# State turned in place by VectorE, S of ten pieces in pairs, spreading on 256 columns: one change to a chunked attention and two feed-forward layers

## The chip, the core and the metric

The kernel runs on one core of a Trainium2 chip. Its engines work side by side, each through its own list of instructions in order: TensorE (PE; its weight loads are a row of their own, PEld), VectorE (DVE), ScalarE (ACT), GpSimd (POOL) and SyncE (SP, which here only starts DMA transfers). Semaphores tie the lists together. Matrix products are written to PSUM, which has eight banks of 512 fp32 columns; everything else lies in SBUF. The metric is the time of the whole program on the device in microseconds (us), lower is better.

## The reference, cut to what matters

```python
def _attn_ref(x, a, B, C):            # x [4, 8, 768, 32], a [4, 8, 768], B, C [4, 8, 768, 16]
    ...
    for c in range(nc):               # chunks along the sequence
        ...
        L = np.exp(cum[:, :, :, None] - cum[:, :, None, :]) * causal
        CB = np.einsum('bhin,bhjn->bhij', Cc, Bc)
        y_intra = np.einsum('bhij,bhjd->bhid', CB * L, xc)
        y_inter = np.einsum('bhin,bhnd->bhid', Cc, state) * decay_to_i[:, :, :, None]
        ...
        state = decay_full[:, :, None, None] * state + np.sum(Bx, axis=2)

def _moe_ref(x, w_in, w_out):         # x [3072, 256], w_in [256, 2048], w_out [2048, 256]
    h = x @ w_in
    return (h * (1.0 / (1.0 + np.exp(-1.702 * h)))) @ w_out

def _moe2_ref(x, w_in, w_out):        # the same shapes
    h = x @ w_in
    return (h * np.clip(h + 3.0, 0.0, 6.0) / 6.0) @ w_out
```

The output of the attention (4 x 768 tokens of 8 x 32 numbers) goes through the first feed-forward layer and its result through the second.

## The kernel before

**Attention in pieces.** The sequence is cut into 8 chunks of 96 positions; a piece q is one chunk c = q // 4 of one batch row b = q % 4, so there are 32. Each has eight heads, in two groups g of four. The state is carried by 16 extra columns and rows: E = 96 + 16 = 112. A piece needs, for each g: the decays `l` of 112 x 448 (a scan on DVE, L406); the products C times B, called S (`s_mm`, L477: four small matmuls for each g), into one PSUM bank per g; their product `gm` (L480 on DVE, or ACT's copy L483 and POOL's product L487); and then y (`y_mm`, L498: eight matmuls over `gm` and `xs`, the piece's x with the state below it in rows 96 to 111). ACT copies the state's part of y to `st_sb` (L502) and the rest to `xt` (L512); DVE adds what the fp32r copy lost (L516).

**S.** For pieces 0 to 15 the operands of S have 16 rows in fp32. Each g and each batch row of a pair lies at its own 32 partitions (`r = 64 * (b % 2) + 32 * g`), and one piece's two groups are issued in turn. Later pieces have 128 rows in bf16.

**Spreading.** For pieces 0 to 5 the decays' factors come from one fp32 tile of 128 x 224 (`acl`): a matmul whose left operand is one column, repeated 112 times, spreads one row over all partitions (`a_spread`, L394), four such matmuls for a piece, into the `acc` banks. For later pieces a DMA does it (L400).

**State from chunk to chunk.** After a chunk's last piece DVE turns the whole `st_sb` in blocks of 32 x 32 into `st_tr` (L523), and four DMAs of 16 KB carry it to rows 96 to 111 of the next chunk's `xs` (`st_move`, L527).

**The two layers.** The 3072 tokens make six blocks of 512 columns. A unit is one block k, one layer (A or B) and one slice m of 128 of the 2048 hidden numbers, 192 in all. A unit has 12 fp32r matmuls of 512 columns: six for h (L659: the weights' high parts `wh`, then their low parts `wl`) and, two units later, six into two `acc` banks (L698). Block 0 needs pieces 0 to 5. Pieces 6 to 15 run between the units of A0 and A1, the rest later.

**Weights.** 32 slices of 512 KB come packed as 64-bit numbers (`raw`, three buffers, L303); ACT scales them (L309) and makes their low bits (L315), DVE joins them (L321), ACT rounds to `wh` (L324), POOL subtracts to `wl` (L330).

**PSUM.** `h` has 2 banks, `acc` 4, `s` and `y` one each. Pieces 0 to 5 use the two `h` banks for S.

**Order.** Every operation is entered with an engine, an estimated duration, a key (its due time) and the buffers that it reads and writes. `Schedule.run` replays the estimates, takes buffers from the pools in the order of the keys, and so fixes the order of the instructions on each engine. `START` is the due time of the first unit, `PIECE` that of each piece. All DMAs except six at the start are issued by SP, in order, and each of those waits for its own condition at the head of the queue.

Of the kernel before, what the change touches and what calls it, by code (L numbers as in the profile page):

```python
# [22 lines left out]
CH = 96  # L23
# [15 lines left out]
DECB = 2  # L39
SPREAD = 6  # L40
KEEP = ((21, 4), (26, 5))
LAG = 2
START = 25.0
# [11 lines left out]
def SBANK(q, g):  # L55
    if q < 6:
        return f"h:s{q}.{g}"
    return f"{('s', 'y' if 8 <= q < 16 else 'acc')[g]}:s{q}.{g}"


def YBANK(q):
    return f"{'ysysys'[q] if q < 6 else 's' if 8 <= q < 16 else 'y'}:y{q}"


def PIECE(q, lead):

# [150 lines left out]
def ssd_moe_kernel(ctx: ExitStack, tc: tile.TileContext, xs, aa, bc, bcz_d, bc0, wu, pat, idn, out):  # L217
# [23 lines left out]
    w_hi = [const.tile([128, UW], F32R, name=f"wh{p}") for p in range(2 * NM)]  # L241
# [7 lines left out]
    eye2 = late_p.tile([128, NH], F32, tag="eye2", name="eye2")  # L249
# [9 lines left out]
    xs_b = bufs("xs", 2, [E, NB, NH * D], F32)  # L259
# [41 lines left out]

    def w_load(p):
        nc.sync.dma_start(out=B_(f"raw:{p}").rearrange("p n t -> p (n t)"), in_=wu[p].bitcast(U32))  # L303

    def w_scale(p):


        top = B_(f"raw:{p}")[:, :, 1].bitcast(F32)
        nc.scalar.activation(top, top, AF.Prelu, scale=2.0 ** 16, alpha=2.0 ** 32)  # L309

    def w_low(p, act):
        low = B_(f"raw:{p}")[:, :, 0]
        if act:

            nc.scalar.activation(low, B_(f"raw:{p}").bitcast(U8)[:, :, 3], AF.Copy, scale=1 / 32, bias=-31 / 64)  # L315
        else:
            nc.vector.tensor_scalar(low, low, 29, None, ALU.logical_shift_right)

    def w_join(p):
        t = B_(f"raw:{p}")  # L320
        nc.vector.scalar_tensor_tensor(B_(f"dec:{p}"), t[:, :, 1], 3, t[:, :, 0], ALU.logical_shift_left, ALU.bitwise_or)  # L321

    def w_top(p, e):
        (e.copy if e is nc.scalar else e.tensor_copy)(w_hi[p], B_(f"dec:{p}").bitcast(F32))  # L324
# [15 lines left out]
    def more_eye():  # L340

        nc.gpsimd.tensor_tensor(out=eye2, in0=idn_sb[:, 0:NH], in1=idn_sb[:, NS + 1:NS + 2].to_broadcast([128, NH]), op=ALU.mult)
# [22 lines left out]
    add("POOL", 0.2, -30, more_eye, r=["idn"], w=["eye2"])  # L365
    add("-", 0.0, -95, lambda: None, w=["late"])
# [8 lines left out]

    def a_all():
# [6 lines left out]

    def a_store():
        nc.sync.dma_start(out=acl_d.rearrange("r (q f) -> (r q) f", q=4), in_=acl())

    def a_spread(q, g):

        f = acl()
        ps = B_(f"acc:l{q}.{g}")[0:E, 0:4 * E]  # L390
        for i in range(2):
            j = 4 * q + 2 * g + i
            row = idn_sb[:, NS + NH + j:NS + NH + j + 1] if j < NS else eye2[:, j - NS:j - NS + 1]
            nc.tensor.matmul(out=ps[:, 2 * E * i:2 * E * i + 2 * E], lhsT=row.to_broadcast([128, E]),  # L394
                             rhs=f, start=True, stop=True)
# [7 lines left out]
    def decay(q, g):  # L403
        t = B_(lname(q)).rearrange("p h e -> p (h e)")[:, 4 * E * g:4 * E * g + 4 * E]
        a = B_(f"acc:l{q}.{g}")[0:E, 0:4 * E] if q < SPREAD else t
        nc.vector.tensor_tensor_scan(t, a, pat_sb, 0.0, ALU.mult, ALU.add)  # L406
# [58 lines left out]
    def s_mm(q, gs):  # L465
        c, b = divmod(q, NB)
        for k in range(4):
            for g in gs:
                ps = s_bank(q, g)
                if c in ROWS:  # L470
                    t = rows16(c)
                    r, i = 64 * (b % 2) + 32 * g, 4 * (b // 2) + k
                    l, r = t[r:r + NS, 0, i], t[r:r + NS, 1, i]
                else:
                    t = B_(f"st:{c}.{b // 2}").rearrange("p (h s b e) -> p h s b e", h=NH, s=2, b=2)
                    l, r = t[:, 4 * g + k, 0, b % 2], t[:, 4 * g + k, 1, b % 2]
                nc.tensor.matmul(out=ps[:, k, :], lhsT=l, rhs=r, start=True, stop=True)  # L477
# [14 lines left out]
    def y_mm(q):  # L492
        c, b = divmod(q, NB)
        yv, x = y_view(q), B_(f"xs:{c}")
        for g in range(2):
            for k in range(4):
                h = 4 * g + k
                nc.tensor.matmul(out=yv[32 * k:32 * k + 32, g, :], lhsT=x[:, b, h * D:(h + 1) * D],  # L498
# [23 lines left out]
    def st_turn():  # L522
        nc.vector.transpose(st_tr.rearrange("p b g e -> p (b g e)"), st_sb.rearrange("p b g e -> p (b g e)"))  # L523
# [297 lines left out]
```

## Time and profile before

| | |
|---|---|
| runs | 602.7, 604.74, 605.6 us; median 604.74 |
| profiled execution | 602.65 us, of which the span of its instructions is 600.5 |
| PE busy | 590.2 us, 98% of the span |
| ACT, DVE, POOL busy | 315.9, 283.5, 196.2 us |
| units: matmuls of 512 columns | 2304 |
| first unit's first matmul | 29.58 us after the span's start |

"Busy" is time in which an engine has an instruction in it. A matmul's recorded length overlaps the next one's, so what one matmul takes is read from the distance between the starts of two. "Idle before" names what ended an engine's wait. [...]

### The profile page before, as it was taken

To read this page: it belongs to the slowest core of one execution; us is meant where nothing else is said; L and a number is where in the kernel's file an instruction comes from. 1 tells how busy PE (TensorE), PEld (TensorE's weight loads), DVE (VectorE), ACT (ScalarE), POOL (GpSimd) and SP (SyncE) were. 2 spreads that over 40 slices of the span, in tenths; PEclk is the share of its full clock that TensorE was granted. 3 is DMA by queue.
4 is the path that set the end of the run, shared out by engine and by line. 5 is a ranking of instruction groups with operands and counts; after the bars stand their busy time and mean duration, and the time that the engine had idled before them with its cause. 6 is when DMAs were issued, how large, how long until landed. Compare 5 with 4: busy or idle time off the path is not lost.

```text
span 600.5 us, 8563 instructions
## 1 busy us (share of the span) xinstructions
PE 590.2 (98%) x3260; PEld 473.4 (79%) x3260; DVE 283.5 (47%) x404; ACT 315.9 (53%) x594; POOL 196.2 (33%) x161
## 2 busy tenths in 40 slices
PE   8799999999999999999999999999999999999997
PEld 6577778778888887777788888778888888888885
DVE  5786776554443454685642364633322222322221
ACT  2478756667767545455344554434544443544443
POOL 3343420124443635463000573000445000444542
PEclk9989999999999999999999999999999999999999
DMA  8386650432231567468340060420000100000101
GB/s 172 110 258 203 207 146 29 137 107 78 99 106 52 145 177 180 148 172 235 104 142 1 11 165 19 137 62 1 1 0 1 35 1 1 0 2 0 37 0 35
DMA packets 46808, 52.82 MB, mean 88 GB/s; under 512 B 26784, under 2 KB 38416, under 8 KB 46768
## 3 DMA queue, kind: packets, MB, share of 16 engines
q1 hardware_dynamic: 45920, 51.93, 30.2%
q10 hardware_dynamic: 848, 0.35, 0.3%
q8 instruction: 25, 0.41, 0.3%
q14 instruction: 15, 0.12, 0.1%
HBM read 41.21 MB, written 10.60 MB: 86 GB/s over the span
## 4 chain that ended last, share of the span: by engine, by line
PE 92%; DMA 4%; ACT 1%; DVE 1%; SPq 0%; issue 0%; POOL 0%; ACTq 0%; DVEq 0%
PE h L659 44%; PE acc L698 43%; PE s L477 2%; PE y L498 2%; DMA raws<-in_wu 1%; PE s L498 1%; DMA xs<-in_xs 1%; DMA out<-gg 1%; DMA late<-in_bcz 1%; PE acc L477 1%; DMA xs<-st_tr 0%; SPq L527 0%; POOL wl L330 0%; DVE l L406 0%; ACT raws L315 0%
## 5 line engine op out<-in xcount | busy, mean ns | idle before, releaser
L684 POOL TENSOR_TENSOR gl<-gg,gh 128x512 fp32r<-128x512 f32 x95 | 126.8, 1338 | 280.6 <-ACT gh L674 262.6
L659 PE MATMUL h<-xt,wh 128*128 128x512 f32 x768 | 211.1, 397 | 0.9 <-DVE xt L516 0.9
L659 PEld LDWEIGHTS h<-xt,wh 128*128 128x128 f32 x768 | 142.9, 189 | 33.5 <-issue 2.1
L698 PE MATMUL acc<-gh,wh 128*128 128x512 f32 x384 | 149.9, 390 | 0.0
L679 DVE SCALAR_TENSOR_TENSOR gg<-gg,h 128x512 f32<-128x512 f32 x96 | 65.8, 685 | 140.6 <-ACT gg L672 140.4
L698 PE MATMUL acc<-gl,wh 128*128 128x512 f32 x384 | 120.3, 389 | 0.0
L684 DVE TENSOR_TENSOR gl<-h,gh 128x512 fp32r<-128x512 f32 x96 | 66.1, 688 | 110.1 <-ACT gh L674 108.6
L670 ACT ACTIVATE h<-h 128x512 f32<-128x512 f32 x96 | 55.9, 582 | 106.9 <-PE h L659 106.8
L698 PE MATMUL acc<-gh,wl 128*128 128x512 f32 x276 | 109.6, 397 | 0.0
L672 ACT ACTIVATE gg<-h 128x512 f32<-128x512 f32 x96 | 57.4, 598 | 82.6 <-PE h L659 77.7
L659 PE MATMUL h<-xt,wl 128*128 128x512 f32 x276 | 86.3, 394 | 0.6 <-POOL wl L330 0.6
L674 ACT CAST gh<-gg 128x512 fp32r<-128x512 f32 x96 | 59.6, 621 | 51.0 <-DVE gg L679 50.9
L698 PEld LDWEIGHTS acc<-gl,wh 128*128 128x128 f32 x384 | 72.1, 188 | 15.5 <-DVE gl L684 0.2
L698 PEld LDWEIGHTS acc<-gh,wh 128*128 128x128 f32 x384 | 72.1, 188 | 14.3
L406 DVE TENSOR_TENSOR_SCAN l<-l,pat_sb 112x448 f32<-112x448 f32 x52 | 66.6, 1290 | 5.1 <-DMA l<-acl_d 5.0
L659 PEld LDWEIGHTS h<-xt,wl 128*128 128x128 f32 x276 | 52.1, 190 | 12.3 <-POOL wl L330 1.0
L698 PEld LDWEIGHTS acc<-gh,wl 128*128 128x128 f32 x276 | 51.8, 188 | 12.4 <-issue 1.5
L330 POOL TENSOR_TENSOR wl<-dec,wh 128x512 fp32r<-128x512 f32 x23 | 32.7, 1428 | 82.7 <-ACT wh L324 82.7
L674 ACT CAST gh<-h 128x512 fp32r<-128x512 f32 x96 | 56.5, 588 | 3.5
L698 PE MATMUL acc<-gh,w_late 128*128 128x512 f32 x108 | 42.4, 392 | 0.0
L659 PE MATMUL h<-xt,w_late 128*128 128x512 f32 x108 | 33.3, 389 | 0.0
L480 DVE TENSOR_TENSOR gm<-s,l 112x448 f32<-112x448 f32 x26 | 16.1, 619 | 17.3 <-PE s L477 8.2
(76 smaller groups left out, 393.1 us busy)
## 6 DMA issues: line engine op xcount, KB each, us to landing
raws<-in_wu SPq DMA_DIRECT2D x21, 512.0 KB, 5.4
l<-acl_d SPq DMA_DIRECT2D x26, 392.0 KB, 5.6
st<-scr SPq DMA_DIRECT2D x8, 896.0 KB, 5.8
raw<-in_wu SPq DMA_DIRECT2D x11, 512.0 KB, 3.4
scr<-tsplit SPq DMA_DIRECT2D x32, 168.0 KB, 2.7
xs<-in_xs SPq DMA_DIRECT2D x8, 384.0 KB, 6.1
scr<-tsplit SPq DMA_DIRECT2D x16, 112.0 KB, 2.6
raw<-in_bc SPq DMA_DIRECT2D x4, 384.0 KB, 5.6
```

Of the source, the lines that this page charges most:

```text
L330: e.tensor_tensor(out=w_lo[p], in0=B_(f"dec:{p}").bitcast(F32), in1=w_hi[p].bitcast(F32), op=ALU.subtract)
L406: nc.vector.tensor_tensor_scan(t, a, pat_sb, 0.0, ALU.mult, ALU.add)
L477: nc.tensor.matmul(out=ps[:, k, :], lhsT=l, rhs=r, start=True, stop=True)
L480: nc.vector.tensor_tensor(out=B_(f"gm:{q}.{g}"), in0=s_bank(q, g), in1=B_(lname(q))[:, 4 * g:4 * g + 4], op=ALU.mult)
L498: nc.tensor.matmul(out=yv[32 * k:32 * k + 32, g, :], lhsT=x[:, b, h * D:(h + 1) * D], rhs=B_(f"gm:{q}.{g}")[:, k, :], start=True, stop=True)
L659: nc.tensor.matmul(out=ps, lhsT=w[p][:, 128 * j:128 * j + 128], rhs=x[:, xp, j, 0:n], start=not lo and (xp, j) == (1, 0), stop=lo and j == 1)
L670: nc.scalar.activation(ps, ps, AF.Gelu_apprx_sigmoid)
L672: nc.scalar.activation(B_(f"gg:{u}")[:, 0:n], ps, AF.Relu, bias=3.0)
L674: nc.scalar.copy(B_(f"gh:{u}")[:, 0:n], ps if kind == "A" else B_(f"gg:{u}")[:, 0:n])
L679: nc.vector.scalar_tensor_tensor(out=g, in0=g, scalar=6.0, in1=B_(f"h:{u}")[:, 0:n], op0=ALU.min, op1=ALU.mult)
L684: e.tensor_tensor(out=B_(f"gl:{u}")[:, 0:n], in0=g, in1=B_(f"gh:{u}")[:, 0:n].bitcast(F32), op=ALU.subtract)
L698: nc.tensor.matmul(out=acc[d], lhsT=w[p][:, 256 + 128 * d:384 + 128 * d], rhs=g, start=(m == 0 and d not in seen), stop=(m == NM - 1 and d ...
```

## The change

Four things, and what goes with them:

- **The state is turned in place.** `xs` gets 128 partitions. For each half of a chunk (two pieces) DVE turns four blocks of 32 partitions of `st_sb` straight into rows 96 to 127 of the next chunk's `xs`: eight small turns for a chunk where one large turn and four DMAs were. `y_mm` reads rows 0 to 111.
- **S of pieces 6 to 15 in pairs.** `s_mm` takes two pieces, (6,7) to (14,15), and issues their four groups in turn: four different sets of rows, four banks (`s`, `y`, two `acc`). For this the odd piece's S is made with the even one's, and its y alternates between `y` and `s`. Pieces 0 to 5 keep the `h` banks.
- **Spreading on 256 columns.** DVE splits `acl` into an fp32r part and a remainder, each padded by POOL to 256 columns; each row is spread by two fp32r matmuls of 256 columns that add up. POOL makes the fp32r selectors from the constants.
- **Early weights.** Four more raw buffers (`early`, the place of the last eight `wh`) take slices 3 to 6; slices 0 to 6 get earliest times `WAFTER`. `START` goes from 25 to 21, which moves the due times of units and weights.

`HALVES`, `PATQ`, `LOWPS` and their branches are switched off (no unit is halved, no pattern copied). The order of the 192 units stays.

```diff
-START = 25.0
+START = 21.0
...
     if q < 6:
         return f"h:s{q}.{g}"
-    return f"{('s', 'y' if 8 <= q < 16 else 'acc')[g]}:s{q}.{g}"
+    if q < 16:
+        return f"{('sy', ('acc', 'acc'))[q % 2][g]}:s{q}.{g}"
+    return f"{('s', 'acc')[g]}:s{q}.{g}"
...
+EARLY = 8
+WAFTER = (2.9, 4.9, 6.9, 11.0, 13.0, 15.0, 17.0)
+PAIRS = (6, 8, 10, 12, 14)
...
+    def a_part(i):
+        t = B_("gh:acl")[:, 256 * i:256 * i + 2 * E]
+        f = acl()
+        if i:
+            nc.vector.tensor_tensor(out=t, in0=f, in1=B_("gh:acl")[:, 0:2 * E].bitcast(F32), op=ALU.subtract)
+        else:
+            nc.vector.tensor_copy(t, f)
...
-            nc.tensor.matmul(out=ps[:, 2 * E * i:2 * E * i + 2 * E], lhsT=row.to_broadcast([128, E]),
-                             rhs=f, start=True, stop=True)
+            for part in range(2):
+                nc.tensor.matmul(out=ps[:, 2 * E * i:2 * E * i + 256], lhsT=sel[:, j:j + 1].to_broadcast([128, E]),
+                                 rhs=B_("gh:acl")[:, 256 * part:256 * part + 256], start=part == 0, stop=part == 1)
...
-    def s_mm(q, gs):
-        c, b = divmod(q, NB)
+    def s_mm(qs, gs):
         for k in range(4):
-            for g in gs:
+            for q in qs:
+                c, b = divmod(q, NB)
+                for g in gs:
...
-    def st_move(c, k):
-        dst = B_(f"xs:{c + 1}")[CH:E].rearrange("n b (g k d) -> n k (b g) d", g=2, k=4)
-        nc.sync.dma_start(out=dst[:, k], in_=st_tr[32 * k:32 * k + NS].rearrange("n b g d -> n (b g) d"))
+    def st_turn(c, j, k):
+        dst = B_(f"xs:{c + 1}")[CH:128, 2 * j:2 * j + 2].rearrange("n b (g k d) -> n k (b g) d", g=2, k=4)
+        nc.vector.transpose(dst[:, k], st_sb[32 * k:32 * k + 32, 2 * j:2 * j + 2].rearrange("p b g e -> p (b g) e"))
...
-        if b == 3 and c + 1 < NC:
-            add("DVE", 0.45, t + 2.5, st_turn, r=[f"st_sb{i}" for i in range(NB)], w=["st_tr"])
+        if b % 2 and c + 1 < NC:
+            for k in range(4):
+                add("DVE", 0.22, t + 2.4 + 8 * (q == 3), st_turn, c, b // 2, k, r=[f"st_sb{b - 1}", f"st_sb{b}", f"xs:{c + 1}"], w=[f"xs:{c + 1}.{b // 2}.{k}"])
```

Three places show how the instructions move. In the names, the number behind an underscore is the tile's own and differs between the two programs.

SP at the start, from the first `xs` on. Before:

```order
L409 DMA xs_141<-in_xs 96x1024
L409 DMA xs_142<-in_xs 96x1024
L385 DMA acl_d<-gg_147 128x224
L449 DMA late<-in_bc 16x1792 x4
L303 DMA raw_130<-in_wu 128x1024
L303 DMA raws<-in_wu 128x1024 x2
L527 DMA xs_142<-st_tr 16x8x32 x4
L400 DMA l_136<-acl_d 112x896
```

And now:

```order
L453 DMA xs_134<-in_xs 96x1024
L324 DMA raw_123<-in_wu 128x1024
L425 DMA acl_d<-gg_140 128x224
L324 DMA raws<-in_wu 128x1024
L493 DMA late<-in_bc 16x1792 x4
L453 DMA xs_135<-in_xs 96x1024
L324 DMA raws<-in_wu 128x1024
L324 DMA early<-in_wu 128x1024 x4
L440 DMA l_129<-acl_d 112x896
```

Weight 0 stands ahead of the B and C of chunk 1 (`late<-in_bc`) and of the second `xs`, weight 1 ahead of both; four more weights follow at once, where the four `xs<-st_tr` stood, which are gone.

ACT at the start, after the table's load. `gm` is the copy of S (for POOL's product), `st_sb` and `xt` are the copies of y, `raw`, `raws` and `early` the weights. Before:

```order
L483 COPY gm_138<-h_159 112x448
L483 COPY gm_140<-h_158 112x448
L502 COPY st_sb<-y_165 128x2x16
L512 CAST xt_144<-y_165 128x2x96
L483 COPY gm_138<-h_159 112x448
L502 COPY st_sb<-s_164 128x2x16
L512 CAST xt_144<-s_164 128x2x96
L309 ACTIVATE raw_130<-raw_130 128x512
L315 ACTIVATE raw_130<-raw_130 128x512
L309 ACTIVATE raws<-raws 128x512
```

And now, first the beginning:

```order
L528 COPY gm_131<-h_152 112x448
L330 ACTIVATE raw_123<-raw_123 128x512
L340 ACTIVATE raw_123<-raw_123 128x512
L547 COPY st_sb<-y_158 128x2x16
L557 CAST xt_137<-y_158 128x2x96
L528 COPY gm_133<-h_151 112x448
L330 ACTIVATE raws<-raws 128x512
L340 ACTIVATE raws<-raws 128x512
L528 COPY gm_131<-h_151 112x448
```

and then the end of it, up to the copies of pieces 4 and 5:

```order
L330 ACTIVATE early<-early 128x512
L340 ACTIVATE early<-early 128x512
L330 ACTIVATE early<-early 128x512
L340 ACTIVATE early<-early 128x512
L547 COPY st_sb<-y_158 128x2x16
L557 CAST xt_137<-y_158 128x2x96
L352 CAST wh_73<-dec_126 128x512
L330 ACTIVATE early<-early 128x512
L547 COPY st_sb<-s_157 128x2x16
L557 CAST xt_137<-s_157 128x2x32
```

Weight 0's two steps stood behind the copies of piece 1 and now stand ahead of those of piece 0; weights 3, 4 and the first step of 5 stand ahead of the copies of pieces 4 and 5.

PE at the first S behind the units' start. Before, piece 6 alone, in two banks:

```order
L659 MATMUL h_159<-xt_144,wl_107 128x512 x2
L477 MATMUL s_164<-late 112x112
L477 MATMUL acc_162<-late 112x112
L477 MATMUL s_164<-late 112x112
L477 MATMUL acc_162<-late 112x112
```

And now pieces 6 and 7, in four:

```order
L751 MATMUL acc_154<-gl_147,wh_74 128x512
L522 MATMUL s_157<-late 112x112
L522 MATMUL y_158<-late 112x112
L522 MATMUL acc_155<-late 112x112
L522 MATMUL acc_156<-late 112x112
```

Two groups in turn have become four, and piece 7's own S further on is gone.

## Rows read from the trace of the kernel before

**Rows 1.** The page: the span, the granted clock in 40 slices.
```profile
span 600.5 us, 8563 instructions
PEclk9989999999999999999999999999999999999999
```

**Rows 2.** The page: busy us of each engine, share of the span, instructions.
```profile
PE 590.2 (98%) x3260; PEld 473.4 (79%) x3260; DVE 283.5 (47%) x404; ACT 315.9 (53%) x594; POOL 196.2 (33%) x161
```

**Rows 3.** Chain of waits up to 31 us and from 40: start, us, what.
```profile
9.80 8.61 DMA raws<-in_wu
...
25.57 1.96 DMA xs<-st_tr
...
45.52 1.36 PE h L659 x6
```

**Rows 4.** Timeline of PE from 10.9 us: start, us, engine line, op, count.
```profile
10.92 1.77 PE L394 MATMUL acc<-gg,idn_sb 128*112 128x224 f32 x8
12.62 1.04 PE L477 MATMUL h<-late 16*112 16x112 f32 x16
13.59 0.59 PE L498 MATMUL s<-gm,xs 112*32 112x112 f32 x16
14.11 1.77 PE L394 MATMUL acc<-gg,idn_sb 128*112 128x224 f32 x8
```

**Rows 5.** Timeline of DVE up to 30 us.
```profile
5.08 2.07 DVE L406 TENSOR_TENSOR_SCAN l<-acc,pat_sb 112x448 f32<-112x448 f32 x2 [1.46 <-PE acc L394]
...
8.78 2.07 DVE L406 TENSOR_TENSOR_SCAN l<-acc,pat_sb 112x448 f32<-112x448 f32 x2 [0.48 <-PE acc L394]
...
22.85 0.33 DVE L516 TENSOR_TENSOR xt<-s,xt 128x192 fp32r<-128x192 f32 x1
23.10 0.43 DVE L523 STREAM_TRANSPOSE st_tr<-st_sb 128x256 f32<-128x256 f32 x1
...
24.43 1.12 DVE L480 TENSOR_TENSOR gm<-h,l 112x448 f32<-112x448 f32 x2
25.48 0.67 DVE L321 SCALAR_TENSOR_TENSOR dec<-raw 128x512 uint32<-128x512 uint32 x1
```

**Rows 6.** Timeline of ACT: the wait for weight 0.
```profile
15.97 0.67 ACT L309 ACTIVATE raw<-raw 128x512 f32<-128x512 f32 x1 [1.32 <-DMA raw<-in_wu]
```

**Rows 7.** Stretches: busy us of PE, PEld, DVE, ACT, POOL, granted clock, DMA, GB/s.
```profile
0.00:10.00 10.00, 8.27 (x54) 6.18 (x56) 4.25 (x7) 2.02 (x3) 3.13 (x9) 1.00 0.78 153
10.00:20.00 10.00, 10.00 (x120) 8.02 (x116) 8.38 (x12) 4.64 (x13) 2.67 (x3) 1.00 0.80 211
30.00:40.00 10.00, 10.00 (x34) 7.48 (x33) 7.33 (x9) 6.65 (x13) 2.27 (x2) 0.75 0.98 287
```

**Rows 8.** Timeline of PE from the first unit to 42.5 us: S of piece 6 within.
```profile
29.58 2.07 PE L659 MATMUL h<-xt,wh 128*128 128x512 f32 x4 [0.87 <-DVE xt L516]
...
34.89 1.26 PE L659 MATMUL h<-xt,wh 128*128 128x512 f32 x4
...
39.19 1.07 PE L659 MATMUL h<-xt,wh 128*128 128x512 f32 x4
...
41.53 0.34 PE L477 MATMUL s<-late 16*112 16x112 f32 x1
...
42.31 0.26 PE L477 MATMUL acc<-late 16*112 16x112 f32 x1
42.50 1.20 PE L659 MATMUL h<-xt,wh 128*128 128x512 f32 x4
...
43.99 0.39 PE L698 MATMUL acc<-gh,wl 128*128 128x512 f32 x1
```

**Rows 9.** Timeline of PEld in the same S: the weight loads.
```profile
42.02 0.17 PEld L477 LDWEIGHTS s<-late 16*112 16x112 f32 x1
42.02 0.17 PEld L477 LDWEIGHTS acc<-late 16*112 16x112 f32 x1
```

More of the change, by code (lines that the diff above doesn't have):

```diff
@@ L364, in ssd_moe_kernel @@
     add("POOL", 0.3, -90, zero_state, w=["st_sb"])
-    add("POOL", 0.2, -30, more_eye, r=["idn"], w=["eye2"])
-    add("-", 0.0, -95, lambda: None, w=["late"])
+    add("POOL", 0.35, -75, selectors, r=["idn"], w=["sel"])
+    add("-", 0.0, -95, lambda: None, w=["late", "early"])
     add("ACT", 0.1, -91, consts, 1, w=["pat"], kb=100)
@@ L405, in decay, with pat_copy @@
         a = B_(f"acc:l{q}.{g}")[0:E, 0:4 * E] if q < SPREAD else t
-        nc.vector.tensor_tensor_scan(t, a, pat_sb, 0.0, ALU.mult, ALU.add)
+        m = B_("acc:pat")[0:E, 0:4 * E] if SPREAD <= q < PATQ else pat_sb
+        nc.vector.tensor_tensor_scan(t, a, m, 0.0, ALU.mult, ALU.add)
+    def pat_copy():
+        nc.scalar.copy(B_("acc:pat")[0:E, 0:4 * E], pat_sb)
     def x_load(c):
@@ L543, in ssd_moe_kernel @@
         add("POOL", 0.3, t + 0.5, identities, s, r=["idn", "split0"], w=[f"split{s + 1}"])
+    if PATQ > SPREAD:
+        add("ACT", 0.55, kp[SPREAD - 1], pat_copy, r=["pat"], new=["acc:pat"])
     for q in range(NC * NB):
@@ L580, in ssd_moe_kernel @@
         if b == 0 and c > 0:
-            add("SP", 0.4, t - 12, x_load, c, new=[f"xs:{c}"], kb=393)
-        if b == 0 and c > 0:
-            for k in range(4):
-                add("SP", 0.4, t - 3, st_move, c - 1, k, r=["st_tr", f"xs:{c}"], w=[f"xs:{c}.{k}"], kb=16)
+            add("SP", 0.4, t - 12, x_load, c, new=[f"xs:{c}"], kb=393, after=8.0)
         if q < SPREAD:
@@ L587, in ssd_moe_kernel @@
             for g in range(2):
-                add("PE", 0.75, t - 1 + 0.1 * g, a_spread, q, g, r=["gg:acl", "idn", "eye2"], new=[f"acc:l{q}.{g}"])
+                add("PE", 0.48, t - 1 + 0.1 * g, a_spread, q, g, r=["gh:acl", "al", "sel"], new=[f"acc:l{q}.{g}"])
             for g in range(2):
@@ L593, in ssd_moe_kernel @@
             for g in range(2):
-                add("DVE", 1.06, t + 0.1 * g, decay, q, g, r=[lname(q), "pat"] + ["late"] * (q == 3), w=[f"l{q}.{g}"], port=True)
+                add("DVE", 1.06, t + 0.1 * g, decay, q, g, r=[lname(q), "acc:pat" if q < PATQ else "pat"], w=[f"l{q}.{g}"], port=q >= PATQ)
         for g in range(2):
@@ L687, in l2 @@
     def l2(u):
-        kind, k, m = order[u]
-        n = WID[k]
+        kind, k, m, a, b = order[u]
+        n = b - a
         p = m + (NM if kind == "B" else 0)
         hi, lo = B_(f"gh:{u}")[:, 0:n], B_(f"gl:{u}")[:, 0:n]
-        acc = [B_(f"acc:{kind}{k}.{d}")[:, 0:n] for d in range(2)]
+        acc = [B_(f"acc:{kind}{k}.{d}")[:, a:b] for d in range(2)]
         seq = [(d, w, g) for d in range(2) for w, g in ((w_lo, hi), (w_hi, hi))] + [(d, w_hi, lo) for d in range(2)]
@@ L741, in ssd_moe_kernel @@
         acc = [f"acc:{kind}{k}.{d}" for d in range(2)]
-        add("PE", 6 * mm(k), tu[u + LAG] + 0.6, l2, u, r=W + [f"gh:{u}", f"gl:{u}"], **({"new": acc} if m == 0 else {"w": acc}))
+        add("PE", 6 * mm(n), tu[u + LAG] + 0.6, l2, u, r=W + [f"gh:{u}", f"gl:{u}"], **({"new": acc} if m == 0 and lo == 0 else {"w": acc}))
         if m == NM - 1:
```

159 lines of the change are left out of this document (93 added, 66 removed).

## The prediction

> **What bounds the kernel now.** I read the page first: the span is 600.5 us [rows 1], and TensorE has an instruction in it for 98% of it [rows 2]. A share of busy time doesn't say that PE runs at its pace, so the timeline and the chain of waits come next. Six matmuls of 512 columns take 1.36 us where nothing disturbs them [rows 3], 0.227 each; 2304 of them are 522 us. What lies beside that is what a change can take: a start of 29.58 us before the first unit [rows 8], the pieces' own matmuls, and a few waits. The rest of the span is PE at its pace, so there work that is taken off PE is time gained, and work added to the other engines costs only where PE comes to wait for it.
>
> The start has three limits that lie close together. On PE one piece takes 3.19 us from one spreading to the next: 1.70 spreading, 0.97 S, 0.52 y [rows 4]. On DVE it takes two scans (2.07 with overlap, 2.0 net), one product (0.53) and one remainder (0.25), 2.8 us [rows 5]. And ACT, in order, stands still for weights: weight 0 lands at 15.97 [rows 6], weight 1 at 18.41 [rows 3], and the copies of y and S behind them wait too. At the end comes the state: y of piece 4 needs the four DMAs that carry it, and the last of them lands at 27.53, 2.0 us after DVE's last product of piece 5 [rows 3, 5]. Then the first two units run at the granted clock 0.50: from 29.58 to 34.89 they take 5.31 us [rows 8] instead of 2 x 1.36, 2.6 lost; the clock is 0.75 over 30 to 40 us [rows 7] and 1.0 in nearly every slice after that [rows 1].
>
> **The change part by part. The start.** The DMAs of the state go, and those 2.0 us with them; the spreading gets shorter. A spread row takes two matmuls of 256 columns where it took one fp32 matmul of 224 (two records of 0.21). No row shows 256 columns in fp32r; they cost between half of 0.227 (0.113) and the whole, and I take 0.12, since the columns set a matmul's pace in rows 3 and 4. Then a piece's eight take about 1.15 us instead of 1.70, and PE needs 2.65 us for a piece: DVE is last.
>
> So I add up DVE. The first scan began at 5.08 [rows 5]. Two instructions are new ahead of the first spreading (a cast and a subtraction of 224 columns, some 0.3 each by the remainder's 0.33); the first four matmuls are shorter: 5.3. Up to the last product of piece 5 come 12 scans of 1.0, seven products of 0.53, four remainders of 0.25, two joins of 0.6 (moved ahead; 0.67 with overlap) and four turns. A turn of 32 x 128 isn't in the trace; the large one took 0.43 for 256 columns [rows 5], so it costs between 0.2 and 0.43; I take 0.2, by the columns. That is 12.0 + 3.7 + 1.0 + 1.2 + 0.8 = 18.7: 24.0 if DVE never waits.
>
> It will wait, through ACT. Weight 0 is issued three transfers earlier: 112 KB, 448 KB and 384 KB now come behind it, which at the 211 GB/s of 10 to 20 us [rows 7] is 4.5 us, so it lands at 11.5 instead of 15.97. But its two steps stand on ACT ahead of the copies of piece 0's y and piece 1's S. S of piece 2 then begins at 13.6, and DVE stands some 0.8 us for piece 0's remainder and 0.4 for piece 2's product, then 0.3 or so twice: 1.6 in all, 25.6 for the last product. Behind it come y of piece 5 (0.5), piece 4's remainder, four more turns, a join and piece 5's remainder: 27.4. ACT reads the same: weight 2 lands where it did (before 20.2), weights 3, 4 and 5 follow at 512 KB each, at 211 to 287 GB/s 1.8 to 2.4 us apart, so 5 lands near 26; its first step (0.6) and the copy of piece 5's y (0.3) end at 27.0, the remainder at 27.3. **First unit at 27.5: 2.1 us gained.** The bounds: 26.0 with no wait on DVE; 31.9 if weights come at the 153 GB/s of the first 10 us [rows 7], which puts weight 5 at 30.2.
>
> The half clock behind it I leave as it is, 2.6 us: PE has even less to do between S of piece 5 and the first unit than before. Bounds 0 and twice that.
>
> **Pairs of S.** One piece's S takes 0.97 us, and the unit behind it 1.49 from 42.50 to 43.99 instead of 1.36 [rows 8]: 1.10 in all, ten times. Inside, two groups start together, every 0.1 us eight times [rows 8], and so do their weight loads [rows 9]. With four sets of rows the eight rounds should stay, with four matmuls in each. Y is the nearest case that has four at once (four sets of columns): 16 records in 0.52 us [rows 4], four every 0.13. I take 1.13 for a pair, so 2.20 - 1.13 = 1.07 saved, five times: **5.3 us**. If only two go at once, there are 16 rounds: 1.10 + 0.78 = 1.88, 0.3 saved, 1.6 in all.
>
> [...] No run here shows four row tiles yet.
>
> **Early weights.** The fourth unit's first layer took from 39.19 to 41.53, 2.34 us instead of 1.36, since its `wl` was late [rows 8]. Weight 3 lands near 22 now instead of behind the state's DMAs at SP's head. **1.0 us gained**; the later waits for weights are too small to see.
>
> **What is added elsewhere.** Eight turns for one in each of seven chunks, 8 x 0.2 - 0.43 = 1.2 us of DVE for a chunk; after the start DVE has the slack (47% busy over the span [rows 2]), so nothing. S of piece 11 is now made with piece 10's, ahead of A1's first two units, and holds two `acc` banks until DVE has multiplied it; A1's second layer needs those banks. PE gets there some 51 us after the first unit with DVE's work up to that product at about 42 us: it fits, but in order, so I charge **0.5 us** (0 to 2). SP loses 28 transfers; the queue behind them only gets earlier.
>
> **The sum.** -2.1 - 5.3 - 1.0 + 0.5 = -7.9 us. Against the profiled execution: 602.65 - 7.9 = 594.8. That execution is 2.1 us below the median of 604.74, and it is the median that I forecast: 604.74 - 7.9 = **596.8 us**.
>
> **Rivals.**
>
> *ACT's queue is held by the weights.* Weights 3, 4 and 5 now stand ahead of the copies that the first unit needs; before, ACT's waits for weights 0 and 1 were on the chain up to the first unit [rows 3, 6]. At 153 GB/s the first unit starts at 31.9, 2.3 later than before instead of 2.1 earlier: 601.2; somewhat faster transfers give 599 to 601. For it: rows 6. Against it: 287 GB/s between 30 and 40 us, when weights made most of the traffic [rows 7]. I say 600.
>
> *The pairs don't do what they say:* two groups at a time, from the rows of the array or from the weight loads, of which the trace shows two every 0.1 us and never more [rows 9]. 1.6 instead of 5.3: 600.5.
>
> *The clock falls inside the start,* because PE now waits there. It stayed at 1.00 while PE was 83% and 100% busy [rows 7]. If it falls at about 18 us, S of piece 5 and y of pieces 4 and 5 take twice as long on the way to the first unit, some 1.5 us: 598.3. [...]
>
> *Slower: the four loads of a round go in line.* If each held the array for its whole recorded 0.17 us [rows 9], a pair would take 32 x 0.17 + 0.13 = 5.6 instead of 2.2: 17 us more in five pairs, 619. It decides from 0.08 us a load (a pair of 2.7), where it eats the other gains. Against it: two loads fit in 0.1 us now.
>
> **How the numbers follow.** Chances: the forecast 0.60, ACT held 0.17, pairs of two 0.10, clock 0.09, loads in line 0.04. About 0.5% (3 us, below 601.7) is what a measurement of this kernel can tell from no change. The forecast and the clock are faster; of ACT held and the pairs of two about a fifth ends above 601.7. So faster 0.90, same 0.06, slower 0.04. The range: at the low end a first unit at 26.0 and a half clock that costs 1 us less with no wait at A1, 593.8, and a base like the lowest run, 2.0 less: 592; at the high end the two middle rivals with a little over: 601.5.
>
> **What would show each step.** Right: first unit near 27.5; a pair's S in about 1.0 us from its first matmul to the next unit's, four starts in each round; the fourth unit in 1.4 us; no wait of PE at A1's first second-layer matmul. Wrong: ACT's L330 waiting for `early` while the copies of pieces 4 and 5 stand behind it; rounds of 0.2 us; a granted clock of 0.5 before the last S.

## The result, and the profile after

| | before | after |
|---|---|---|
| median of the timed runs | 604.97 us (602.7 to 605.6) | 595.74 us (595.59 to 596.08) |
| ratio | | 0.9862, 95% interval 0.9832 to 0.9892 |
| profiled execution, its span | 602.65 us, 600.5 us | 595.59 us, 593.8 us |

The changed kernel is 1.4% faster. The kernel before was timed again beside the experiments below, with medians of 603.6 to 604.3 us, so times taken apart can be compared only to about 1 us.

The page of the changed kernel, beside [rows 1, 2]:

```profile
span 593.8 us, 8567 instructions
PE 582.0 (98%) x3260; PEld 468.6 (79%) x3260; DVE 301.5 (51%) x455; ACT 316.8 (53%) x594; POOL 201.3 (34%) x163
PEclk9689999999999999999999999999999999999999
```

PE has 8 us less to do and is as full as before. DVE has 18 us more, most of it the turns. PEclk is the clock granted to TensorE in 40 slices, in tenths of full speed: six matmuls of 512 columns took 2.72 us in a stretch at 0.50 (28.25 to 30.97) and 1.36 in one at 1.00 (36.03 to 37.39). In the second slice (14.8 to 29.7 us) it is at 0.6 where it was at 0.9. So the next view is the start, on PE (start, us, line, op, count, and in brackets the idle time before it and who ended it):

```profile
17.97 1.31 PE L522 MATMUL h<-late 16*112 16x112 f32 x16
...
22.17 1.91 PE L522 MATMUL h<-late 16*112 16x112 f32 x16 [1.99 <-DVE gm L525]
24.01 0.97 PE L543 MATMUL y<-gm,xs 112*32 112x112 f32 x16
...
28.25 2.08 PE L712 MATMUL h<-xt,wh 128*128 128x512 f32 x4 [1.80 <-DVE xt L561]
...
33.19 1.19 PE L712 MATMUL h<-xt,wh 128*128 128x512 f32 x4
```

The first unit starts at 28.25 us, 1.3 earlier than in [rows 8]. S of piece 5 takes 1.9 us instead of 1.0: the clock is at half already. The first two units take 4.94 us, 5.31 before. The stretches of the same profile (us, busy time of five engines, granted clock, DMA share, GB/s) say when it fell:

```profile
10.00:20.00 10.00, 9.56 (x144) 7.52 (x140) 9.70 (x17) 5.19 (x14) 3.42 (x3) 0.95 1.04 281
20.00:30.00 10.00, 5.72 (x56) 4.11 (x53) 9.43 (x19) 8.62 (x21) 6.56 (x6) 0.50 1.04 313
```

0.95 over ten us is 1.0 up to 19.1 and 0.5 from there. DMA moves 281 and 313 GB/s here, against 211 in [rows 7], so the weights come sooner than I had charged. DVE is full, 9.4 of 10 us, and its row up to the first unit is

```profile
24.04 0.62 DVE L525 TENSOR_TENSOR gm<-h,l 112x448 f32<-112x448 f32 x1
...
25.71 0.35 DVE L561 TENSOR_TENSOR xt<-y,xt 128x192 fp32r<-128x192 f32 x1
26.07 1.26 DVE L570 STREAM_TRANSPOSE xs<-st_sb 32x128 f32<-32x128 f32 x4
27.36 0.69 DVE L346 SCALAR_TENSOR_TENSOR dec<-raws 128x512 uint32<-128x512 uint32 x1
27.97 0.41 DVE L561 TENSOR_TENSOR xt<-s,xt 128x64 fp32r<-128x64 f32 x2
28.90 2.17 DVE L447 TENSOR_TENSOR_SCAN l<-l,pat_sb 112x448 f32<-112x448 f32 x1
```

Four turns take 1.26 us, 0.32 each. They and a join stand ahead of the remainder (27.97) that the first unit waits for.

A pair of S and the fourth unit, on PE:

```profile
36.03 1.07 PE L712 MATMUL h<-xt,wh 128*128 128x512 f32 x4
...
37.39 0.39 PE L751 MATMUL acc<-gh,wl 128*128 128x512 f32 x1
...
41.56 0.34 PE L522 MATMUL s<-late 16*112 16x112 f32 x1
41.57 0.34 PE L522 MATMUL y<-late 16*112 16x112 f32 x1
41.58 0.35 PE L522 MATMUL acc<-late 16*112 16x112 f32 x2
...
42.35 0.26 PE L522 MATMUL acc<-late 16*112 16x112 f32 x2
42.55 1.20 PE L712 MATMUL h<-xt,wh 128*128 128x512 f32 x4
...
44.04 0.39 PE L751 MATMUL acc<-gh,wl 128*128 128x512 f32 x1
```

Four matmuls start within 0.02 us, and the last four start 0.77 us behind the first: 32 in 0.99 us where one piece's 16 took 0.97 [rows 8]. The fourth unit's first layer takes 1.36 us. And at A1's start there is something new:

```profile
74.17 1.20 PE L712 MATMUL h<-xt,wh 128*128 128x512 f32 x4 [0.53 <-DVE xt L561]
...
75.67 1.07 PE L712 MATMUL h<-xt,wh 128*128 128x512 f32 x4
...
77.85 1.21 PE L712 MATMUL h<-xt,wh 128*128 128x512 f32 x4 [0.66 <-DVE gl L737]
...
79.36 1.09 PE L712 MATMUL h<-xt,wh 128*128 128x512 f32 x4
...
80.74 0.39 PE L751 MATMUL acc<-gh,wl 128*128 128x512 f32 x1
```

Four first layers in a row, and two waits; against PE's pace they lose 0.7 and 0.8 us, 1.5 in all.

The account on PE: first unit -1.3, the next two units -0.4, fourth unit -1.0, pairs 5 x (1.10 + 1.10 - 1.12) = -5.4, A1's start +1.5: -6.6 of the -6.7 us between the two spans.

### The profile page after: what moved, and what is told of

It is laid out like the page before. It is cut to its first block, busy times and chain, and to the rows that moved or that the text cites. A ratio compares the mean times of both kernels' runs of the same rounds, so it can differ in the third digit from the quotient of the medians.

```text
span 593.8 us, 8567 instructions
## 1 busy us (share of the span) xinstructions
PE 582.0 (98%) x3260; PEld 468.6 (79%) x3260; DVE 301.5 (51%) x455; ACT 316.8 (53%) x594; POOL 201.3 (34%) x163
## 4 chain that ended last, share of the span: by engine, by line
PE 94%; DMA 2%; ACT 1%; DVE 1%; issue 0%; SPq 0%; DVEq 0%; ACTq 0%
PE h L712 45%; PE acc L751 44%; PE y L543 2%; PE s L522 1%; DMA raw<-in_wu 1%; DMA late<-in_bcz 1%; DMA out<-gg 1%; PE h L522 1%; PE acc L522 1%; PE s L543 1%; DVE l L447 0%; DVE xt L561 0%; PE acc L434 0%; ACT gg L725 0%; DVE dec L346 0%
## 5 line engine op out<-in xcount | busy, mean ns | idle before, releaser
L737 POOL TENSOR_TENSOR gl<-gg,gh 128x512 fp32r<-128x512 f32 x95 | 128.6, 1356 | 277.8 <-ACT gh L727 255.7
L712 PE MATMUL h<-xt,wh 128*128 128x512 f32 x576 | 159.3, 399 | 3.2 <-DVE xt L561 2.3
L712 PEld LDWEIGHTS h<-xt,wh 128*128 128x128 f32 x576 | 107.1, 190 | 28.6 <-DVE xt L561 3.2
L751 PE MATMUL acc<-gh,wh 128*128 128x512 f32 x288 | 112.4, 390 | 0.0
L751 PE MATMUL acc<-gl,wh 128*128 128x512 f32 x288 | 89.7, 389 | 0.0
L447 DVE TENSOR_TENSOR_SCAN l<-l,pat_sb 112x448 f32<-112x448 f32 x52 | 68.7, 1331 | 9.5 <-DMA l<-acl_d 9.4
L751 PEld LDWEIGHTS acc<-gl,wh 128*128 128x128 f32 x288 | 54.1, 188 | 11.5
L751 PEld LDWEIGHTS acc<-gh,wh 128*128 128x128 f32 x288 | 54.1, 188 | 10.8
L712 PE MATMUL h<-xt,w_early 128*128 128x512 f32 x192 | 52.0, 392 | 0.0
L751 PE MATMUL acc<-gh,w_late 128*128 128x512 f32 x108 | 42.5, 393 | 0.0
L712 PEld LDWEIGHTS h<-xt,w_early 128*128 128x128 f32 x192 | 35.6, 188 | 7.2 <-issue 0.2
```

The source lines that it names most:

```text
L447: nc.vector.tensor_tensor_scan(t, a, m, 0.0, ALU.mult, ALU.add)
L712: nc.tensor.matmul(out=ps, lhsT=w[p][:, 128 * j:128 * j + 128], rhs=x[:, xp, j, a:b], start=not lo and (xp, j) == (1, 0), stop=lo and j == 1)
L737: e.tensor_tensor(out=B_(f"gl:{u}")[:, 0:n], in0=g, in1=B_(f"gh:{u}")[:, 0:n].bitcast(F32), op=ALU.subtract)
L751: nc.tensor.matmul(out=acc[d], lhsT=w[p][:, 256 + 128 * d:384 + 128 * d], rhs=g, start=(m == 0 and a == 0 and d not in seen), stop=(m == N ...
```

## The experiments

Each run is the changed kernel (595.74 us) with one edit, unless it says otherwise.

**Two groups at a time.** Only the order of the 32 matmuls inside a pair changes:

```
-        for k in range(4):
-            for q in qs:
+        for q in qs:
+            for k in range(4):
```

> The changed kernel with one edit: inside a pair's burst the 16 matmuls of the first piece stand ahead of the 16 of the second, so that only two row groups can go at a time; order on every other engine is the same. Theory (the gain of the pairs is four row groups side by side in eight rounds): a pair's S takes about 1.8 us from its first matmul to the next unit's instead of 1.0, five pairs cost 0.8 us each, 4.0 us in all, 599.7 us against 595.7. Rival (the gain is that one burst of 32 replaces two bursts, each with its own late unit behind it): a pair keeps about 1.0 to 1.3 us, and the time is within 1 us of the changed kernel.

597.92 us (0.9902, 0.9886 to 0.9918): 2.2 us lost, between the two. On PE a pair of this run:

```profile
41.66 0.34 PE L522 MATMUL s<-late 16*112 16x112 f32 x1
...
42.15 0.35 PE L522 MATMUL acc<-late 16*112 16x112 f32 x2
42.23 0.26 PE L522 MATMUL s<-late 16*112 16x112 f32 x1
...
42.44 0.75 PE L522 MATMUL acc<-late 16*112 16x112 f32 x11
43.12 1.20 PE L712 MATMUL h<-xt,wh 128*128 128x512 f32 x4
```

1.46 us a pair, 0.47 more, five times 2.35. The second piece (`acc`) does not wait for the first to end: its first matmuls start at 42.15, halfway through, although matmuls of the first piece that stand ahead of them in PE's list start only at 42.23 and later. So of the 1.08 us that a pair saves, some 0.5 come from the interleaved order and 0.6 from the two bursts being one. My 0.8 had taken the two for strictly serial.

**No pairs.**

```
-PAIRS = (6, 8, 10, 12, 14)
+PAIRS = ()
```

with the banks of the kernel before for pieces 6 to 15.

> The changed kernel without pairs: S of pieces 6 to 15 one by one, in the banks of the kernel before; turns, spreading and early weights stay. Theory: ten singles of 1.10 us (0.97 and 0.13 in the unit behind) instead of five pairs of about 1.1, +5.3 us, and the 1.5 us of waits at A1's start, which I put down to the turns on VectorE and not to the pair of pieces 10 and 11, stay: 601 us. Rival (the waits at A1's start come from the pair that holds two accumulator banks): they go, and the time is 599.5 us. Second rival (pairs are worth nothing): 596 us.

600.85 us (0.9950, 0.9935 to 0.9964), 5.1 above the changed kernel. The first expectation has the time, but not by its sum: A1's waits are gone, which is the rival's sign, and the profiled execution has a worse start:

```profile
10.00:20.00 10.00, 9.54 (x109) 7.47 (x106) 7.34 (x14) 4.44 (x13) 2.28 (x2) 0.71 1.04 271
```

The clock fell at 14.2 us, and the first unit starts at 30.80, 2.55 later than in the changed kernel, with the instructions up to there in the same order. So the time alone does not price the pairs. Of the 7.0 us between the two profiled spans (600.8 and 593.8), 2.55 lie at the first unit and A1's start gives 1.5 back, which leaves 5.9 for ten single S instead of five pairs; the rows of one pair gave 5.4. The ten runs lie between 600.28 and 604.36, the profiled one at 602.57, so where the clock falls may be worth 2 us and more from one execution to the next.

**The state by DMA.** One turn of 128 x 256 and four transfers for a chunk, as before:

```
-                add("DVE", 0.22, t + 2.4 + 8 * (q == 3), st_turn, c, b // 2, k, ...)
+            add("DVE", 0.45, t + 2.5, st_turn, ..., w=["st_tr"])
+                add("SP", 0.4, t - 3, st_move, c - 1, k, r=["st_tr", f"xs:{c}"], ...)
```

> The changed kernel with the state carried as in the kernel before: one turn of 128 x 256 for each chunk and four DMAs through SyncE's queue in place of the eight turns of 32 x 128; spreading, pairs and early weights stay. Theory: the chain to the first unit gets 2.0 us of DMA between the last state's copy and y of piece 4 and loses 1.0 us of turns on VectorE, so the first unit starts between 28.8 and 30 us instead of 28.25, and A1's start loses about 0.5 us of its waits: net +0.5 to +1.5 us, 596.2 to 597.2 us. Rival (the turns cost VectorE as much as the DMAs cost the chain): within 0.4 us of the changed kernel or faster.

597.75 us (0.9892, 0.9877 to 0.9907), 2.0 lost. On PE:

```profile
26.54 1.32 PE L543 MATMUL y<-gm,xs 112*32 112x112 f32 x15 [1.17 <-DMA xs<-st_tr]
...
30.60 2.07 PE L715 MATMUL h<-xt,wh 128*128 128x512 f32 x4 [1.81 <-DVE xt L561]
```

The wait for the transfers is back, and the first unit is 2.35 us later than with the turns in place, more than the 0.6 to 1.8 that I had expected. The four transfers take 4.2 us from issue to landing (median), 1.9 in the kernel before; here weights 4 to 6 were still on their way, up to 26.3 us. At A1's start this run has no wait, and PE's own row shows what differs:

```profile
71.85 1.20 PE L715 MATMUL h<-xt,wh 128*128 128x512 f32 x4
...
73.34 0.39 PE L754 MATMUL acc<-gh,wl 128*128 128x512 f32 x1
...
76.82 1.09 PE L715 MATMUL h<-xt,wh 128*128 128x512 f32 x4
...
79.57 0.39 PE L754 MATMUL acc<-gh,wl 128*128 128x512 f32 x1
```

First layers stand one or two together here, with second layers between, although the pairs and their banks are those of the changed kernel.

**The spreading of the kernel before.** One fp32 matmul of 224 columns for a row, no cast and no subtraction:

```
-            for part in range(2):
-                nc.tensor.matmul(out=ps[:, 2 * E * i:2 * E * i + 256], ...)
+            nc.tensor.matmul(out=ps[:, 2 * E * i:2 * E * i + 2 * E], ..., rhs=acl(), ...)
```

> The changed kernel with the spreading of the kernel before: one fp32 matmul of 224 columns for a row (two records of 0.21 us) in place of two of 256 in fp32r, and without the cast and the subtraction on VectorE ahead of it. Theory (VectorE sets the pace of the start, so shorter spreading on TensorE brings little): PE needs 0.6 us more for a piece, 3.2 against VectorE's 2.8 to 3.1; the first unit 0.5 to 1.5 us later, and 0.3 us of it comes back with the two steps that go: 596 to 597 us. Second part of the theory: with longer matmuls on PE the granted clock stays at 1.0 past 19 us in the profile, as it did in the kernel before. Rival (PE's spreading was on the path in every piece): six times 0.6, 3.6 us later, 599.3 us.

597.36 us (0.9901, 0.9885 to 0.9917), 1.6 lost, a little over the range. In the profile the first unit starts at 28.95, 0.7 later, and the rest is at A1's start, where the planner's order changed again. Here the clock was at 1.0 up to 26.7 us, as the second part said; what that proves is limited by the spread of the run without pairs.

**No early weights.** Three buffers instead of seven:

```
-        return f"{'rawe' if 3 <= p < 3 + EARLY // 2 else 'raw'}:{p}"
+        return f"raw:{p}"
```

> The changed kernel with the three buffers for raw weights that the kernel before had, so that weights 3 to 6 wait for a buffer; turns, pairs and spreading stay. Theory (early weights are worth the wait of the fourth unit, 1.0 us, and nothing else): 596.7 us, with the fourth unit at 2.3 us instead of 1.36 in the profile. Rival (their steps on ScalarE hold up the copies in the start as much as they give): 595.2 to 596.0 us.

599.77 us (0.9946, 0.9928 to 0.9964): 4.0 lost, where either side had at most 1.0. And the sign that the theory named did not come. The fourth unit's first layer takes 1.36 us here too:

```profile
36.98 1.07 PE L712 MATMUL h<-xt,wh 128*128 128x512 f32 x4
...
38.34 0.39 PE L751 MATMUL acc<-gh,wl 128*128 128x512 f32 x1
...
55.10 1.16 PE L712 MATMUL h<-xt,wh 128*128 128x512 f32 x4 [2.04 <-DVE gl L737]
```

Weight 3 goes into the buffer of weight 0, which came early too, and lands at 23.8 us; in the kernel before it landed at 32.3. The first unit is 0.9 later, and the next four keep that distance. Then 2.2 us go ahead of 55.10, where PE waits for a product behind a scan of 3.5 us on DVE, and 1.5 us right behind it, where the granted clock is 0.50 from 56.4 to 59.8 us. How much of that is the weights and how much another order from the planner isn't settled.

**The start reordered by dependencies.** Extra entries in the read lists make the planner place certain steps behind others, among them

```
-            r=[f"acc:l{q}.{g}", lname(q), "pat"] + ["late"] * (q == 3), ...
+            r=[f"acc:l{q}.{g}", lname(q), "pat"] + ["late"] * (q == 3) + ["gm:4.0"] * (q == 4 and g or q == 5), ...
```

> The changed kernel with the same instructions in another order, by hand: on VectorE the product of piece 4 ahead of its second scan, the joins of weights 1 and 2 and the four turns for pieces 6 and 7 behind the products and the remainder that the first unit waits for, the four turns at A1's start behind the remainder of piece 10; on ScalarE the steps of weights 0, 2 and 4 on behind the copies of the pieces. Theory (the 1.5 us at A1's start and some 2 us of the start are order on VectorE and ScalarE alone): first unit at 26.2 to 27 us in the profile, no wait of TensorE for a remainder at A1's start, 592.5 to 594 us. Rival (VectorE is as late with any order, or the clock's fall moves onto the units): within 0.5 us of the changed kernel.

597.07 us (0.9905, 0.9875 to 0.9936): not faster. The four runs took 595.6, 595.9, 598.3 and 598.7 us; the profile is of the second, and what the two longer ones lost in addition is not shown. In it the first unit started at 26.22, and PE still waited for a remainder at A1's start (0.92 us), which the theory had gone. What the start won was lost at one place; DVE, then POOL, then PE:

```profile
43.52 5.32 DVE L447 TENSOR_TENSOR_SCAN l<-l,pat_sb 112x448 f32<-112x448 f32 x2
```

```profile
43.47 1.29 POOL L358 TENSOR_TENSOR wl<-dec,wh 128x512 fp32r<-128x512 f32 x1 [1.74 <-ACT wh L352]
44.72 1.95 POOL L532 TENSOR_TENSOR gm<-gm,l 112x448 f32<-112x448 f32 x1
46.62 1.26 POOL L358 TENSOR_TENSOR wl<-dec,wh 128x512 fp32r<-128x512 f32 x1
```

```profile
49.56 1.16 PE L712 MATMUL h<-xt,wh 128*128 128x512 f32 x4 [2.49 <-DVE gl L737]
```

Two scans that read SBUF take 5.3 us where two take 2.1 elsewhere (2.08 at 353.94 in the changed kernel). They lie beside three two-operand instructions of POOL, and the product that PE waits for stands behind them.

**Dummy matmuls for the clock.** Two of 448 columns ahead of y of each of the first six pieces, six ahead of the first unit:

```
+        if q < 6:
+            dummies(B_(yname[q]), 2)
```

> The changed kernel with dummy matmuls (bf16, 448 columns, on a constant, into a bank that is written over afterwards): two ahead of y of each of the first six pieces, and six ahead of the first unit. Theory (the granted clock of 0.5 from 19.07 to 32.72 us costs about 2.2 us in the first two units, and PE's small bursts are what let it fall): if the clock holds at 1.0 the first two units take 2.7 us instead of 4.94 and the time is 593.5 us; the dummies of 0.19 us each lie in PE's waits for VectorE. Rival (the clock falls anyway, or PE becomes the last one in the start): no gain, 595.5 to 597.5 us.

595.69 us (0.9858, 0.9835 to 0.9881), four runs at 594.36, 594.52, 596.87 and 596.88. In the profile of the first one:

```profile
20.00:30.00 10.00, 8.32 (x83) 4.36 (x83) 9.77 (x19) 8.93 (x21) 6.30 (x7) 0.83 1.04 314
```

The clock held up to 24.8 us and was back at 28.2; the first two units took 3.67 us instead of 4.94, 0.66 of it a wait for DVE. Two runs of four won 1.2 and 1.4 us, two lost 1.1: the rival's "no gain" in the median.

Both together:

> The order of the run before it and the dummy matmuls of the earlier run in TensorE's waits. Theory (the two gains add): the first two units at the full clock, 2.7 us instead of 4.9, and the start as early as without dummies: 590.5 to 592 us. Rival (the granted clock falls in some executions all the same, as the spread of 594.4 to 596.9 us in the earlier run may say): two groups of times some 2.4 us apart, with a median like that of the run without dummies.

597.87 us (0.9918, 0.9895 to 0.9942). It has the loss of the reordered run (a wait of 2.5 us for the same product). The profiled execution was the slowest of the four (599.98): there the clock fell at 19.7 us in spite of the dummies, two of which then took 0.93 us of PE instead of 0.55, the first unit started at 30.04, and the clock fell again at 53.8 us, behind that wait.

**The turns at A1's start moved.** The planner's order stays; four turns go behind two remainders by hand:

```
+    move([('st_turn', 2, 0, 0), ..., ('st_turn', 2, 0, 3)], ('y_lo', 10))
```

> The changed kernel in its own order on every engine, with one move: the four turns of pieces 8 and 9 stand on VectorE behind the two remainders of piece 10 and not ahead of them. Theory (TensorE's first wait at A1's start is those 1.26 us of turns, and the second wait follows from the first, since ScalarE and VectorE start on A1's first unit as late as TensorE does): the wait of 0.93 us shrinks to nothing, the second of 1.05 to 0.5 or less, 594.3 to 594.8 us. Rival (the second wait is VectorE's scans of piece 12 ahead of the unit's product, and the turns now stand ahead of it): the first wait goes and the second grows, 595.5 us.

595.46 us (0.9869, 0.9851 to 0.9887): the rival's. The first wait is gone, the second has grown from 0.8 to 1.46 us against PE's pace, so the sum is the same. Of PE's waits for this product between 24 and 100 us, two and 1.5 us in all, the one at A1's start is the longest:

```profile
PE h L712 <- DVE gl L737: 1.5, 2, 1.3
```

**The start moved too**, with the rest of the order untouched:

```
+    move([('decay', 4, 1)], ('g_mul', 4, 0))
+    move([('w_join', 1)], ('y_lo', 4))
+    move([('st_turn', 0, 1, 0), ..., ('st_turn', 0, 1, 3)], ('y_lo', 5))
+    ...
```

> The changed kernel in its own order, with that move and those of the start alone: on VectorE product 4 ahead of its second scan, the joins of weights 1 and 2 and the turns of pieces 2 and 3 behind the products and remainders of pieces 4 and 5, the first scan of piece 6 behind the first unit's remainder; on ScalarE the steps of weights 0, 2, 4 and 5 behind the copies; the order behind the start, which the planner changed in the reordered run, is that of the changed kernel. Theory (the reordered run won 2.0 us up to the first unit and lost 2.6 us at 46.7 us, where two scans of VectorE from SBUF met GpSimd's products and took 2.2 and 3.2 us instead of 1.1): first unit at 26.2 to 26.6 us, no wait over 1 us between 30 and 70 us, 592 to 593.5 us. Rival (whatever the start wins is given back at the next weights or at the two banks of the units): 594.5 to 595.7 us.

594.76 us (0.9856, 0.9835 to 0.9876). First unit at 26.17, no loss at 46 us, and yet the median is only 1 us lower, which its interval does not tell from the changed kernel. ScalarE and PE show the rest:

```profile
26.25 0.71 ACT L330 ACTIVATE early<-early 128x512 f32<-128x512 f32 x1
...
30.10 0.61 ACT L723 ACTIVATE h<-h 128x512 f32<-128x512 f32 x1
```

```profile
32.11 1.19 PE L712 MATMUL h<-xt,wh 128*128 128x512 f32 x4 [0.91 <-DVE gl L737]
```

The first unit's step on ScalarE (30.10) stands behind five steps of weights 4 to 6 and two roundings. The early start is given back as waits of the third and the fourth unit: the first unit is 2.1 us ahead of the changed kernel's, the fifth (38.56 against 38.75) only 0.2. The other 0.6 us of the 0.8 between the two spans are won later, 0.4 of them between 217 and 231 us, where this edit moves nothing.

> The same with dummy matmuls as in the earlier run (two ahead of y of each of the first six pieces, four ahead of the first unit). Theory: where the granted clock holds at 1.0 up to the first unit, the first two units take 2.7 us instead of 4.9, less what then waits for VectorE: 590.5 to 592 us, and in executions where it falls at 18 to 20 us as without dummies, 592.5 to 594. Rival (the dummies bring nothing in the median): the same median as the run before it.

595.21 us (0.9859, 0.9839 to 0.9878), all runs within 0.9 us: the spread is smaller, the median the same, as the rival said. In the profile the clock held up to 25.9 us and the first unit started at 26.51, but the third waited 1.7 us for its product, and the fifth came 0.2 us behind that of the changed kernel.

**The last version** moves ScalarE's steps as well, keeps the dummies, and sets A1's first product ahead of a scan:

```
+    move([('act', 0, 0), ('act', 0, 1)], ('w_top', 2))
+    move([('w_scale', 5), ('w_low', 5, True)], ('act', 0, 1))
+    move([('decay', 11, 1)], ('g_mul', 11, 0))
+    ...
```

> The moved order with the dummy matmuls, and two more places set by hand: on ScalarE, behind the copies of piece 5, the roundings of weights 1 and 2, then the first unit's two steps, and only then the steps of weights 5 and 6 (those of weight 4 go ahead of piece 5's copies, where ScalarE stands idle); on VectorE at A1's start the product of A1's first unit ahead of the second scan of piece 11 (the expectation of an earlier run called it piece 12). Theory (in the moved runs what the start won was given back because the first unit's steps stood on ScalarE behind two weights, and A1's second wait is that scan): the waits of 2.0 and 1.0 us behind the second and third units of the last profile shrink by 1.5 to 2 us in sum, A1's wait of 1.5 us by 0.6 to 0.9, 592.3 to 593.3 us. Rival (ScalarE has 2.75 us of work for each of these units, as long as TensorE's 2.72, so the next unit waits for what the first one no longer does): 594.3 to 595.2 us.

594.55 us (593.91 to 595.96; 0.9838, 0.9825 to 0.9851), the lowest of all, though its interval overlaps that of the changed kernel. From the first unit to the fourth it took 8.43 us, in the run before 9.61: 1.2 won, a little less than expected:

```profile
27.13 1.96 PE L720 MATMUL h<-xt,wh 128*128 128x512 f32 x4
...
31.96 1.19 PE L720 MATMUL h<-xt,wh 128*128 128x512 f32 x4 [0.23 <-DVE gl L745]
```

The first unit itself came later than in the run before (27.13 against 26.51), and A1's start still loses 1.4 us. There four first layers follow each other and two banks take them in turn: the third needs the product of the first, some 2 us behind its end, and neither of the two orders of DVE tried here made the sum of the waits smaller.

## Why the prediction was right, step by step

The time forecast was 596.8, the time measured 595.74. Within the sum the pairs held, the fourth unit had the right size for a reason that a run took away, and the first unit, the clock and A1's start were off.

- **Pairs: held.** 1.07 us for each pair forecast, 1.08 measured, eight rounds with four in each: 32 matmuls took 0.99 us where 16 took 0.97. The run without pairs has 5.1 us more, though not by the pairs alone.
- **Fourth unit: the size held, the reason only in part.** 1.36 us, 1.0 gained. But the four early buffers are not what gave it: without them weight 3 still landed at 23.8 us and the unit still took 1.36, and with the state by DMA it took 1.36 as well. What the buffers are worth isn't shown: without them 4.0 us were lost, elsewhere. The earlier due times of the weights were not taken back by themselves.
- **First unit: mis-sized.** 2.1 forecast, 1.3 measured. Two durations were off, in opposite directions. A turn of 32 x 128 takes 0.32 us, not 0.2, so two sets cost 1.0 us more of DVE; weights 0 and 3 to 5 came 0.6 to 2.5 us sooner than charged. Up to DVE's last product of piece 5 they cancel (25.6 forecast, 25.7 measured); what stands behind it up to the first unit took 2.5 us instead of 1.9. (A slip without effect: eight spreading matmuls at 0.12 make 0.96, not 1.15; they took 1.11 at 10.98.) The decisive step was the list "four more turns, a join and piece 5's remainder": I summed the work without asking whether the remainder could go first. In the moved run it did, with the products ahead too, and the first unit started at 26.17. That the turns are still the better way shows in the run with the state by DMA (30.60).
- **The clock: the rival with 0.09 came true.** It fell at 19.1 us, inside the start, and S and y of the last pieces ran at half (1.91 and 0.97 us where they took 1.04 and 0.59 at 1.00). The price of 1.5 us did not follow: PE waited for DVE anyway, whose last scan ended at 24.1 while S of piece 5 ended at 24.0. Where the dummies held the clock up to 24.8, the first unit came no earlier (28.60, six dummies ahead of it). In the run without pairs it fell at 14.2, S of three pieces took 1.84 to 1.91 us, ACT waited up to 3.4 us for y on PE, and the first unit was 2.55 us later. So a fall inside the start can cost time there, and the price hangs on the moment. That PE's waits let the clock fall, as the rival has it, is not shown: in the changed kernel PE's row is busy for 4.82 of the 4.90 us just ahead of its fall at 19.1.
- **A1's start: mis-sized, and the place on the wrong engine's row.** 0.5 charged (0 to 2), 1.5 measured. I had weighed a wait of A1's second layer for the banks that piece 11 holds. No such wait came: the planner had set four first layers in a row instead, and the price is PE running dry twice. With second layers between (state by DMA, no pairs) nothing waits; with the turns moved or the product moved the sum stays at 1.4 to 1.5. That the planner did so because of those banks is not shown, and the run with the state by DMA speaks against it: it has the same pairs and banks and no four in a row. The order of PE's rows, which is known before a run, had it in plain sight.
- **The base.** The profiled executions differ by 7.1 us, the medians by 9.2. I had set 7.9 against the median; the sum was 1.2 too large against the spans (6.7) and 1.3 too small against the medians. That the forecast came within 1.1 us of the time is in part luck: the runs of before spread over 3 us.

ACT held by the weights, two groups at a time and loads in line did not occur: ACT never stood for an `early` weight ahead of a copy, and four loads go in a round. But ACT did stand 1.5 us for weight 2, up to 19.64, with the copies of piece 3 behind it, and in the run without early weights, where weight 2 landed 1.0 us later, the first unit came 0.9 later. So the first rival's mechanism is there in small, at a weight that it had not named.

## What to carry to other kernels

Where matmuls use 16 of the array's rows, put those of two independent pieces into one burst and interleave them, so that each round has four sets of rows (here 32 matmuls in 0.99 us, where 16 took 0.97): half of the gain, some 0.6 of 1.08 us a pair, comes from the one burst, half, some 0.5, from the interleaving. Work that is moved from a queue onto a busy engine costs what stands behind it there, so ask of each instruction added whether it must come ahead of the one that the next stage waits for. And a gain at the start lasts only as far as the next engine has slack: in the moved run 2.1 us at the first unit were 0.2 at the fifth, with ScalarE's steps for the next weights ahead of the units' own; setting those behind brought 1.2 us back up to the fourth unit.

## What the runs showed of the hardware

- By the trace's records, TensorE did not start its matmuls in the order of its list. In the run with two groups at a time, with the second piece's 16 behind the first's, the second's began at 42.15 us, ahead of six of the first's (42.23 to 42.44). In the changed kernel four row groups side by side took a round of 0.10 us each (41.76 to 42.35), as long as two in the kernel before (41.72 to 42.31).
- In the changed kernel a scan on VectorE whose operands both lie in SBUF took 1.06 to 1.10 us where no two-operand instruction of GpSimd was under way as it began (30 scans, 1.08 at 42.15), and 1.09 to 2.19 where one was (22 scans, 1.35 at 54.27 and 2.17 at 28.90). The 12 scans that read PSUM took 1.06 to 1.09 us, four of which began with GpSimd in such an instruction: two took 2.06 together at 22.03, with GpSimd in one from 21.79 on. What holds the scans up is not shown.
- The granted clock fell from 1.00 to 0.50 at 19.1 us in the changed kernel and at 14.2 without pairs, though PE's row is nearly full of records of small matmuls there (9.56 and 9.54 of the 10 us from 10 to 20); with the spreading of the kernel before it fell at 26.7. In the first two a full row was no sign that it would hold. With dummy matmuls it fell between 24.8 and 27.3 us in three profiles, and in a fourth at 19.7 all the same.
